# Attention and soft-MoE in one kernel: q and k loaded in four-row pieces plus a rest, in place of nine rows per partition

## The chip, the cores and the metric

One core of a Trainium2 chip runs the whole program. The metric is the device time of one execution in microseconds (us), the median of the runs shown. Beside it stands one execution under the hardware profiler, from which all durations below come.

## What is computed

There are 8 batches and 8 heads, 576 tokens and 16 beacon tokens per head, 64 channels per head. Attention is causal over the tokens, and the 16 beacon keys are open to all of them. Its output, 4608 rows of 512, goes through a soft mixture of experts with 8 experts of 4 slots and an inner width of 1024. Cut to what matters:

```
k_all = concat(beacon_k, k);  v_all = concat(beacon_v, v)        # 16 + 576 tokens
a = softmax(where(causal, -1e9, q @ k_all.T / 8))
x = (a @ v_all), heads side by side                              # (4608, 512)
logits = x @ phi                                                 # (4608, 32)
slot_input = softmax(logits, over tokens).T @ x                  # (32, 512)
slot_out[e] = relu(slot_input[e] @ w1[e]) @ w2[e]                # 8 experts
out = softmax(logits, over slots) @ slot_out                     # (4608, 512)
```

## The kernel before

The work has three stages. In the **attention stage** the loop of line 316 goes over 32 pairs of heads (n). In the **expert stage** (lines 385 to 399) the 32 slots go through the experts' two matrices. In the **output stage** (lines 405 to 420) the slot outputs are spread back over the 4608 rows.

The schedule is written out by hand: each engine runs its instructions in the order of the code. One iteration n of the attention loop issues, in this order: `score(n, 0)` and `score(n, 1)` (scores of pair n, exp on ScalarE at line 209, causal masks on GpSimd at lines 211 and 217), `transp(n + 1)`, `attend(n - 1, 0)`, `score(n, 2)`, `attend(n - 1, 1)`, `score(n, 3)`, up to three pieces of routing of the batch before (transposes of x, logits, slot inputs), then the loads: `load_pair(n + 5)`, a part of the next batch's v (`load_v`), casts of v (`cast_v`, odd chunks on VectorE, even chunks on GpSimd, line 244), and in two of three iterations from n = 3 on one piece of an expert's weights (`load_w`, from GpSimd's queue, line 119).

`load_pair` (line 83) brings q and k of two heads, each into a tile of 128 partitions of 9 rows of 64 fp32 values (`qf`, `kf`; the pool `qkp` has five buffers for each). Partition p holds rows 9p to 9p + 8 of the two heads' 1152 rows, so one DMA of 288 KB with one run of 2304 bytes per partition does it. These loads and those of v and the outputs go through SyncE's queue (SP), one after the other; a load into a buffer waits until TensorE has transposed what was there, five pairs earlier.

`transp` (line 181) takes the upper half of each fp32 value as bf16 and transposes it on TensorE, 18 matmuls of 64x64 for q and 18 for k, into a PSUM tile `tr` of the shape [128, 9, 64] (row within the partition, then partition). Then VectorE copies the tile to `qT` or `kT`, three buffers each, in which the columns are tokens in their natural order (line 190). The token 9s + j stands in PSUM at j * 64 + s, so this copy reads PSUM with a step of 64 elements and writes SBUF without gaps. GpSimd adds the 16 beacon columns to `kT` (line 193). The pool `ps_tr` has two buffers, which the routing pieces use as well.

`attend` (line 222) multiplies the masked exponentials by v and a column of ones, 15 matmuls into `av` (line 230). VectorE takes the reciprocal of the sums (line 237) and scales (line 238, into `xb`). The output tiles `osb` of line 406 use the slots of the weight tiles `w1h`, before and after the change.

Of the kernel before, what the change touches and what calls it, by code (L numbers as in the profile page):

```python
# [17 lines left out]
def kernel(  # L18
# [12 lines left out]
    nc = tc.nc  # L31
    P = 128
    B, H, S, D = q.shape
    Nb = beacon_k.shape[2]
# [7 lines left out]
    J = S // 64  # L42
# [40 lines left out]
    def load_pair(n):  # L83
        b, g = divmod(n, H // 2)
        for (d, src, nm) in ((qf, q, "qf"), (kf, k, "kf")):
            t = qkp.tile([P, J, D], FP, name=nm, tag=nm)
            nc.sync.dma_start(
                out=t[:, :, :],
                in_=src[b, 2 * g:2 * g + 2].rearrange("h s d -> (h s) d").rearrange(
                    "(p j) d -> p j d", j=J))  # L90
            d[n] = t

    vf = {}
# [14 lines left out]
    def load_w(m):  # L108
# [7 lines left out]
        else:  # L116
# [3 lines left out]
            out=d[e][:, o:o + 2048].rearrange("p (c f) -> p c f", c=c), in_=src)  # L120

    load_pair(0)
    bkf = const.tile([P, B, D], FP, name="bkf")
    nc.sync.dma_start(out=bkf[:, :, :], in_=beacon_k.rearrange("b h n d -> (h n) b d"))
    load_pair(1)
    load_v(0, 0)
    load_v(0, 1)
    load_v(0, 2)
    load_v(0, 3)
    phif = const.tile([P, NDC, NSL], FP, name="phif")  # L130
    nc.sync.dma_start(out=phif[:, :, :], in_=moe_phi.rearrange("(c p) e -> p c e", p=P))
    load_pair(2)
    load_pair(3)
    load_pair(4)
# [46 lines left out]
    def transp(n):  # L181
        for (f, dst) in ((qf, qT[n % 3]), (kf, kT[n % 3])):
            t = f.pop(n)
            tp = ps_tr.tile([P, J, 64], BF, name="tr", tag="tr")
            for j in range(J):
                for po in (0, 64):
                    hi = t[po:po + 64, j, :].bitcast(BF)[:, 1::2]
                    nc.tensor.transpose(tp[po:po + 64, j, :], hi,  # L188
                                        idb[po:po + 64, po:po + 64])
            nc.vector.tensor_copy(  # L190
                out=dst[:, Nb:Nb + S].rearrange("p (s j) -> p s j", j=J),
                in_=tp[:, :, :].rearrange("p j s -> p s j"))
        nc.gpsimd.tensor_copy(out=kT[n % 3][:, 0:Nb], in_=bkT[:, n, :])

    ex = {}
# [113 lines left out]
    nc.vector.tensor_copy(out=phih[:, :, :], in_=phif[:, :, :])  # L309
    beacons()  # L310
    transp(0)
    for c in range(NCH):
        cast_v(0, c)
    work = []
    wl = 0
    for n in range(NP + 1):
        b, g = divmod(n, H // 2)
# [4 lines left out]
        if n + 1 < NP:  # L322
            transp(n + 1)
# [81 lines left out]
    for cg in range(NG):  # L405
        osb = wh.tile([P, G, Dm], FP, name="osb", tag="w1h")
        dst = out[cg * P * G:(cg + 1) * P * G, :].rearrange("(p j) d -> p j d", j=G)
# [43 lines left out]
```

The softmax here doesn't subtract the row's maximum and nothing guards it: scores larger than these inputs give would overflow.

## Time and profile before

| what | value |
|---|---|
| runs | 251.77, 255.45, 257.04 us; median 255.45 |
| the profiled execution | 257.04 us, of which the span from first to last instruction is 255.1 us |
| granted TensorE clock, mean | 0.853 of full speed |
| busy share of the span | TensorE 73%, its weight loads 52%, VectorE 52%, ScalarE 50%, GpSimd 34% |
| DMA packets | 63714, 55.63 MB |
| first transposes of pair 0; of pair 31 | at 16.2 us; at 177.7 us |
| expert stage; output stage | from about 196 us; from about 226 us |

The shares of busy time are means over the three stages. Times in the views count from the start of the span. Where a view gives a share of the DMA engines, it is the sum of the times that packets took, divided by 16 engines; packets of one engine overlap in part, so the share can be a little over 1.

### The profile page before, as it was taken

To read this page: it belongs to the slowest core of one execution; us is meant where nothing else is said; L and a number is where in the kernel's file an instruction comes from. 1 tells how busy PE (TensorE), PEld (TensorE's weight loads), DVE (VectorE), ACT (ScalarE), POOL (GpSimd) and SP (SyncE) were. 2 spreads that over 40 slices of the span, in tenths; PEclk is the share of its full clock that TensorE was granted. 3 is DMA by queue.
4 is the path that set the end of the run, shared out by engine and by line. 5 is a ranking of instruction groups with operands and counts; after the bars stand their busy time and mean duration, and the time that the engine had idled before them with its cause. 6 is when DMAs were issued, how large, how long until landed. Compare 5 with 4: busy or idle time off the path is not lost.

```text
span 255.1 us, 8017 instructions
## 1 busy us (share of the span) xinstructions
PE 187.0 (73%) x3512; PEld 132.5 (52%) x3512; DVE 131.4 (52%) x304; ACT 128.3 (50%) x187; POOL 87.2 (34%) x161
## 2 busy tenths in 40 slices
PE   0038877778876777788878798798867999967770
PEld 0036655657755656566666666577566445521110
DVE  6055656755766756664576557556543000035651
ACT  0108677675675666656567556756821000025550
POOL 4024445442454434625244353432460440000000
PEclk9999999997999999779799659958967579985555
DMA  7999779999999999979989999173579999908997
GB/s 218 215 315 256 188 210 247 287 249 236 237 230 215 194 285 233 263 222 231 217 236 206 240 185 268 25 106 61 85 114 202 192 180 202 190 6 364 408 403 301
DMA packets 63714, 55.63 MB, mean 218 GB/s; under 512 B 41920, under 2 KB 50112, under 8 KB 62656
## 3 DMA queue, kind: packets, MB, share of 16 engines
q1 hardware_dynamic: 50880, 38.35, 52.0%
q0 software_dynamic: 12800, 16.78, 40.6%
q8 instruction: 27, 0.44, 0.7%
q14 instruction: 7, 0.06, 0.1%
HBM read 62.46 MB, written 9.44 MB: 282 GB/s over the span
## 4 chain that ended last, share of the span: by engine, by line
PE 54%; DVE 30%; ACT 6%; SPq 3%; issue 3%; DMA 2%
PE av L230 12%; PE tr L188 7%; PE av L397 7%; PE sc_155 L203 6%; PE tr L272 4%; DVE xb_142 L238 4%; PE tr L257 4%; DVE xb_141 L238 4%; PE sc_154 L411 3%; PE sc_154 L203 3%; PE tr L392 3%; DVE osb L415 3%; DVE qT_129 L190 3%; ACT osb L414 2%; ACT ex L209 2%
## 5 line engine op out<-in xcount | busy, mean ns | idle before, releaser
L209 ACT ACTIVATE ex<-sc_154 128x1024 f16<-128x1024 f32 x64 | 63.0, 984 | 41.9 <-PE sc_154 L203 41.8
L211 POOL TENSOR_SCALAR_AFFINE_SELECT ex<-ex 128x1024 f16<-128x1024 f16 x32 | 34.8, 1087 | 86.7 <-ACT ex L209 86.7
L230 PEld LDWEIGHTS <-ex 128*128 128x128 f16 (+2 forms) x960 | 42.8, 113 | 33.1 <-issue 31.6
L209 ACT ACTIVATE ex<-sc_155 128x992 f16<-128x992 f32 x64 | 48.4, 756 | 21.5 <-PE sc_155 L203 21.5
L230 PE MATMUL av<-vh_137,ex 128*128 128x65 f16 (+2 forms) x480 | 24.4, 209 | 11.5 <-DVE xb_141 L238 11.5
L230 PE MATMUL av<-vh_138,ex 128*128 128x65 f16 (+2 forms) x480 | 23.0, 203 | 13.1 <-DVE xb_142 L238 12.2
L397 PE MATMUL av<-w2h,hTz 128*32 128x512 f16 x64 | 18.6, 443 | 2.3 <-ACT hTz L395 2.3
L188 PE MATMUL tr<-idb,kf 64*64 64x64 bf16 x576 | 17.3, 209 | 0.8 <-DVE bkT L175 0.4
L188 PE MATMUL tr<-idb,qf 64*64 64x64 bf16 x576 | 17.5, 211 | 0.0
L188 PEld LDWEIGHTS <-qf 64*64 64x64 bf16 x576 | 13.7, 123 | 7.0 <-issue 5.7
L188 PEld LDWEIGHTS <-kf 64*64 64x64 bf16 x576 | 14.9, 124 | 1.5 <-issue 1.0
L395 ACT ACTIVATE hTz<-tr 128x32 f16<-128x32 f32 x8 | 1.6, 197 | 27.3 <-PE tr L392 27.3
L401 DVE TENSOR_SCALAR soh<-av,rd 32x512 f16<-32x512 f32 x1 | 0.7, 740 | 27.5 <-PE av L397 27.5
L119 POOL DMA_DIRECT2D w1h<-in_moe_w_dram x16 | 11.5, 722 | 9.7 <-PE tr L392 9.7
L411 PEld LDWEIGHTS <-eLh 32*128 32x128 f16 x36 | 4.5, 124 | 18.0 <-issue 17.6
L411 PE MATMUL sc_154<-soh,eLh 32*128 32x512 f16 x18 | 8.6, 576 | 6.9 <-DVE osb L415 6.1
L119 POOL DMA_DIRECT2D w2h<-in_moe_w_dram x16 | 12.0, 756 | 4.4 <-PE av L397 4.4
L190 DVE COPY qT_128<-tr 128x576 bf16<-128x576 bf16 x11 | 8.3, 756 | 9.9 <-PE tr L188 9.8
L190 DVE COPY qT_129<-tr 128x576 bf16<-128x576 bf16 x11 | 8.3, 756 | 8.7 <-PE tr L188 8.6
L190 DVE COPY qT_130<-tr 128x576 bf16<-128x576 bf16 x10 | 7.6, 756 | 9.6 <-PE tr L188 9.6
L172 PE MATMUL tr<-idb,bkd 128*128 128x128 bf16 x8 | 1.0, 311 | 15.3 <-DVE bkd L169 15.3
L414 ACT ACTIVATE osb<-sc_154,rc 128x512 f32<-128x512 f32 x9 | 6.2, 687 | 11.9 <-PE sc_154 L411 11.9
(207 smaller groups left out, 327.7 us busy)
## 6 DMA issues: line engine op xcount, KB each, us to landing
qf<-in_q_dram SPq DMA_DIRECT2D x32, 288.0 KB, 4.7
kf<-in_k_dram SPq DMA_DIRECT2D x32, 288.0 KB, 5.2
w1h<-in_moe_w_dram POOLq DMA_DIRECT2D x16, 512.0 KB, 8.2
w2h<-in_moe_w_dram POOLq DMA_DIRECT2D x16, 512.0 KB, 8.1
out_dram<-osb SPq DMA_DIRECT2D x8, 1024.0 KB, 3.9
vf<-in_v_dram SPq DMA_DIRECT2D x24, 256.0 KB, 6.3
vf<-in_v_dram SPq DMA_DIRECT2D x8, 224.0 KB, 5.4
vf<-in_v_dram SPq DMA_DIRECT2D x8, 160.0 KB, 6.7
```

Of the source, the lines that this page charges most:

```text
L119: nc.gpsimd.dma_start(out=d[e][:, o:o + 2048].rearrange("p (c f) -> p c f", c=c), in_=src)
L188: nc.tensor.transpose(tp[po:po + 64, j, :], hi, idb[po:po + 64, po:po + 64])
L190: nc.vector.tensor_copy(out=dst[:, Nb:Nb + S].rearrange("p (s j) -> p s j", j=J), in_=tp[:, :, :].rearrange("p j s -> p s j"))
L203: nc.tensor.matmul(sc[0:kn, a, col:col + un], kT[n % 3][64 * a:64 * a + 64, P * c:P * c + kn], qT[n % 3][64 * a:64 * a + 64, u0:u0 + un], ...
L209: nc.scalar.activation(ex[n][:, :, o:o + w], sc[:, :, 0:w], AF.Exp, scale=scale)
L211: nc.gpsimd.affine_select(out=ex[n][:, :, 0:512].rearrange("p a (c t) -> p a c t", c=4), in_=ex[n][:, :, 0:512].rearrange("p a (c t) -> p ...
L230: nc.tensor.matmul(av[0:m, a, i * DD:(i + 1) * DD], ex[n][0:kn, a, o:o + m], vh[b % 2][0:kn, c, h, :], start=(c == 0), stop=(c == i))
L238: nc.vector.tensor_tensor(out=xb[b % 2][:, :, h, :], in0=avv[:, :, 0:D], in1=r5[:, :].unsqueeze(2).broadcast_to([P, NCH, D]), op=AL.mult)
L257: nc.tensor.transpose(tp[:, ii, t, 0:m], xb[b % 2][0:m, i, 2 * t:2 * t + 2, :].rearrange("p h d -> p (h d)"), idh[0:m, 0:m])
L397: nc.tensor.matmul(sop[0:NSL, 0, :], hTz[:, e, t, :], w2h[e][:, t * Dm:(t + 1) * Dm], start=(e == 0 and t == 0), stop=(e == E - 1 and t == ...
L411: nc.tensor.matmul(fp_[:, a, :], etok(cg, jj + a), soh[:, :], start=True, stop=True)
L414: nc.scalar.activation(osb[:, jj, :], fp_[:, 0, :], AF.Copy, scale=rc[:, i:i + 1])
```

## The change

Each of q and k of a pair now comes in three DMAs in place of one. The first two bring 512 rows of one head each to 64 partitions: partition p gets rows 4p to 4p + 3 and 256 + 4p to 256 + 4p + 3, two runs of 1 KB. The third brings the last 64 rows of both heads, one row of 256 bytes per partition: on the DRAM side its pattern is 2 heads x 64 rows x 64 values, on the SBUF side 128 partitions x 64 values. The matmuls of the transposes stay the same. The copy out of PSUM becomes two: one of 512 columns, which reads PSUM without gaps in runs of 64 and writes every fourth bf16 element (a step of 8 bytes), and one of the last 64 columns, without gaps on both sides.

```diff
         for (d, src, nm) in ((qf, q, "qf"), (kf, k, "kf")):
             t = qkp.tile([P, J, D], FP, name=nm, tag=nm)
-            nc.sync.dma_start(
-                out=t[:, :, :],
-                in_=src[b, 2 * g:2 * g + 2].rearrange("h s d -> (h s) d").rearrange(
-                    "(p j) d -> p j d", j=J))
+            for a in range(2):
+                hs = src[b, 2 * g + a]
+                nc.sync.dma_start(
+                    out=t[64 * a:64 * a + 64, 0:8, :].rearrange("p (c j) d -> p c j d", j=4),
+                    in_=hs[0:512].rearrange("(c p j) d -> p c j d", p=64, j=4))
+            nc.sync.dma_start(out=t[:, 8, :],
+                              in_=src[b, 2 * g:2 * g + 2, 512:S, :])
             d[n] = t
...
             nc.vector.tensor_copy(
-                out=dst[:, Nb:Nb + S].rearrange("p (s j) -> p s j", j=J),
-                in_=tp[:, :, :].rearrange("p j s -> p s j"))
+                out=dst[:, Nb:Nb + 512].rearrange("p (c s j) -> p c j s", c=2, j=4),
+                in_=tp[:, 0:8, :].rearrange("p (c j) s -> p c j s", j=4))
+            nc.vector.tensor_copy(out=dst[:, Nb + 512:Nb + S], in_=tp[:, 8, :])
```

## The prediction

> **What bounds the kernel now.** I read the page first. Its chain of work that ended last belongs to TensorE and VectorE; DMA has 2% of it.
>
> ```profile
> PE 54%; DVE 30%; ACT 6%; SPq 3%; issue 3%; DMA 2%
> L190 DVE COPY qT_128<-tr 128x576 bf16<-128x576 bf16 x11 | 8.3, 756 | 9.9 <-PE tr L188 9.8
> ```
>
> The chain in order of time shows one pair (columns: start, us, what):
>
> ```profile
> 101.30 0.76 DVE qT_130 L190
> 102.06 0.66 DVE kT_133 L190
> 102.72 0.11 DVE r_2245 L237
> 102.83 0.02 issue
> 102.86 0.50 DVE xb_142 L238
> 103.36 0.04 issue
> 103.40 0.67 PE av L230 x15
> ```
>
> The copies of q and k stand ahead of the reciprocal and the scaling, and the second `attend` waits for the scaling. The waits say that this happens in all 31 such iterations (15 + 16), 23.7 us in total:
>
> ```profile
> PE av L230 <- DVE xb_142 L238: 12.2, 15, 1.0
> PE av L230 <- DVE xb_141 L238: 11.5, 16, 1.0
> ```
>
> So VectorE's copies lie on the path, and loads don't. SP's own waits, and the table of stretches (columns: stretch, us, busy PE, PEld, DVE, ACT, POOL with counts, granted clock, DMA share, GB/s) tell how near the loads are:
>
> ```profile
> SPq L87 <- PE tr L188: 78.7, 25, 5.7
> ```
>
> ```profile
> 20.00:60.00 40.00, 31.51 (x731) 24.87 (x731) 23.99 (x56) 28.15 (x38) 18.42 (x35) 0.97 0.99 240
> 60.00:100.00 40.00, 30.47 (x730) 24.02 (x725) 26.16 (x64) 27.03 (x39) 18.45 (x35) 0.99 1.07 239
> 100.00:140.00 40.00, 33.03 (x747) 26.32 (x743) 24.97 (x58) 26.12 (x38) 17.28 (x33) 0.87 1.00 226
> ```
>
> SP waits for buffers (so loads are ahead), but the last column but one, the DMA engines' share, stands at 0.99 to 1.07: little is free. Part of that is queueing. From the trace's DMA packet records I take service times of one engine: 256-byte packets (v) 19 ns, from the fullest 2.5 us (2,080 packets on 16 engines; median record 18); 2304-byte packets (q, k) 93 ns (median); weight packets 80 ns (w1 and w2 alternate: 503 packets of one kind in 2.5 us) and 155 ns (258 of the other). Mixed full stretches come out at 93 to 100% with these prices.
>
> Work of one engine until the last q/k has landed: q/k 64 tiles x 8 packets x 93 = 47.6 us; v and beacons 38,912 packets / 16 x 19 = 46.2 us; 16 weight pieces issued by then (8 x 32 x 80 + 8 x 16 x 155 ns) = 40.3 us. Sum 134 us of the 158 us between 2 and 160 us. The pairs' transposes start every 5.2 us (16.2 to 177.7 us, 31 steps); the last loads are in some 20 us before use.
>
> [...] Every pattern of the kernel before starts with 128, 112, 80 or 16, all multiples of 16; the trace has no other[...]. [...] copies without gaps out of PSUM take 160, 214, 314 and 687 ns for 32, 128, 320 and 1024 elements (0.53 ns each after some 145 ns), while line 190 with its read step takes 752 ns, 145 + 576 x 1.05. [...]
>
> **The change, part by part.**
>
> VectorE: the 512-element copy writes with a step of 4, so 145 + 512 x 1.05 = 683 ns; the rest 145 + 64 x 0.53 = 179 ns[...]. That is 862 in place of 752 ns busy. But successive instructions overlap by some 75 ns (the copy of q above starts at 101.30 and takes 0.758, that of k starts at 101.97), so on the path a tile costs 608 + 104 in place of 677: +35 ns. Times 62 tiles: +2.2 us, at most 62 x 110 ns = +6.8 us without overlap. [...] TensorE's matmuls are unchanged; the waits for a tile's three DMAs fall on different transposes, and I put them at nothing: covered by loads that are in 20 us early; if late, the whole PE queue behind, `attend` included, stands.
>
> SP: 6 issues per pair for 2, at 0.33 to 0.43 us: +1.6 us per pair of SP, hidden in the 78.7 us of waiting. SP's records show eight completion semaphores used in turn, so at most eight loads are in flight; the pair's 7.25 loads fit its 5.2 us as long as one lands in under 8 / 7.25 x 5.2 = 5.7 us (before: 4.7 to 6.7, for whole tiles). v, next in SP's queue, goes out 1.6 us later; GpSimd already waits three times for its fifth chunk (6.6 us), so 0 to 3 us may come from there. At the start eight more issues precede phi, whose landing at 14.3 us lets VectorE begin: +1 us, up to +2.4 us.
>
> DMA engines: a 1 KB packet lies on the line through 18, 93 and 159 ns (256, 2304, 4096 bytes): 46 ns[...]. The two head loads: 256 packets, 16 per engine, 0.736 us, about what one load costs now (0.744). The rest is the point: 128 packets of 256 bytes with a DRAM pattern that starts with 2. [...] it runs on 2 engines, 64 packets each: 64 x 19 = 1.216 us on those two, nothing on the others. (Spread over 16 it would be 0.152 us.)
>
> So the two engines have to do, until the last q/k: 64 x (0.736 + 1.216) = 124.9, v 46.2, weights 40.3: 211.4 us in place of 134. Start at 2, landing about 1 us after the last packet: 214.4 us. It is consumed at 177.7 in the kernel before: +36.7 us. Per pair: 2 x 1.952 + 1.44 + 1.68 = 7.0 us against the 5.2 us at which TensorE consumes. The lead of five pairs lasts until about pair 9 (loaded at 2 + 5 x 3.9 + 6.7 for the first v, + 2 x 5.35 + 3 x 7.0 = 60 us; its transposes start at 59 us). From there on VectorE's +35 ns are hidden under waiting for loads (left: ten pairs, under 1 us). What follows the last pair (18 us of attention tail, experts, outputs) stays. [...] two groups of line 397 take 3.6 us where the granted clock is low and 1.9 where it is high, so I take off 3 us.
>
> Sum against the profiled execution: span 255.1 + 36.7 - 3 = 289, 257.04 gives 291. The median of the runs is 1.6 us lower: 255.45 + 34 = 289; I say 288. [...]
>
> **Rivals.**
>
> A, the rest spreads over 16 engines[...] Then the start (+2.4), VectorE (+2.2) and late v (+2) give 262. [...]
>
> B, not slower: the rest spreads over 16 engines[...]: 64 x 0.888 + 46.2 + 40.3 = 143 us, hidden. Left are VectorE's 2.2 and the start's 1: 258.5. It decides at the number of engines that the rest uses: the room is 178 - 3 - 134 = 41 us, the rest takes 155.6 / k us, so from k = 4 on it is hidden. For it: every DMA in this trace uses 16. Against: the pattern of DRAM can't be merged, as the heads are 576 rows apart.
>
> C, faster: [...] (145 + 271 = 416 ns): on the path 341 + 104 for 677, 62 x 232 ns = 14 us less, with loads hidden: 241. Against: step 4 on the write side.
>
> **How the numbers follow.** The likeliest 0.66 at 288, own range 264 to 303; A 0.09 at 262; B 0.20 at 258.5, 256 to 262; C 0.05 at 241. What a measurement of this kernel can tell from no change is about 2%, 5.1 us: 250.3 to 260.6. Slower by over 2%: 0.66 + 0.09 + 0.05 of B = 0.80; within: 0.15 of B; faster: 0.05. The range leaves out C, the lower part of B and the top of the likeliest: 258 to 303.
>
> **What would show it.** In the profile after: waits of `tr` (line 188) for DMA `qf`/`kf`, from about pair 9 on, of over 1 us per pair; transposes some 6.5 to 7 us apart in the second half; the last near 214 us; the DMA share in these stretches well under 1, as 14 engines idle; two copies of some 680 and 180 ns in line 190. Wrong if `tr` doesn't wait for DMA at all (B), if the large copy takes near 420 ns (C), or if the wait is there with the DMA share at 1 (A).

## The result and the profile after

The changed kernel takes 314.97 us, the median of 4 runs (313.11 to 317.47), beside 255.76 us for the kernel before (4 runs, 251.77 to 257.04). The ratio is 1.243, with a 95% interval of 1.221 to 1.264. Ratios with an interval, here and below, are taken from the undisturbed executions alone, so they differ a little from the quotients of the medians. The profiled execution took 314.24 us, its span 312.3 us against 255.1. In this section "after" is that execution.

Where the 57.2 us lie, read from the starts of the transposes as in the prediction: the first comes at 20.95 us instead of 16.22 (+4.7), the pairs are 6.88 us apart instead of 5.21 (31 steps, +51.7), and what follows the last start takes 78.2 us instead of 77.4 (+0.8). So nearly all is in the attention loop.

The page's chain of work that ended last has moved from TensorE towards VectorE and DMA, and the copies are two kinds (the columns after the bar: busy us, mean ns, idle before):

```profile
PE 40%; DVE 36%; DMA 10%; SPq 4%; ACT 4%; issue 3%; POOL 1%
...
L193 DVE COPY qT_148<-tr 128x512 bf16<-128x512 bf16 x11 | 14.4, 1309 | 10.9 <-PE tr L191 10.8
```

The copy of 512 columns takes 1309 ns; the copy of all 576 took 756. The chain in order of time shows a pair after the change (start, us, what):

```profile
142.17 0.64 PE tr L191 x18
142.81 0.02 issue
142.83 1.30 DVE qT_148 L193
144.14 0.03 DVE qT_148 L196
144.16 1.14 DVE kT_151 L193
145.30 0.02 DVE kT_151 L196
145.33 0.05 DVE r_2483 L241
145.38 0.02 issue
145.40 0.50 DVE xb_161 L242
145.90 0.04 issue
145.94 1.04 PE av L234 x15
```

The sequence is that of the pair that the prediction shows, but the two copies hold the path for 1.30 + 0.03 + 1.14 + 0.02 = 2.49 us where they held it for 0.76 + 0.66 = 1.42. The rest copies (L196, 221 ns each) overlap the next instruction almost wholly. The second thing to see is the last line: the 15 matmuls take 1.04 us where before's chain has 0.67, with the same instructions.

Summed over the loop, from the first transposes of pair 0 to those of pair 31, the chain has 74.1 us of copies of q and k where it had 31.1 (+43.0), 95.8 us of TensorE where it had 88.6 (+7.2), and 9.9 us of waiting for v where it had none; its other parts shrank. So in the changed kernel itself most of what the path gained lies in the copies.

The waits (times in us: total, count, longest) show the lengthened wait for the scaling, and a grown one, of GpSimd for v. First GpSimd's of the kernel before, then those after the change:

```profile
POOL vh_137 L244 <- DMA vf<-in_v_dram: 5.2, 2, 3.9
...
POOL vh_138 L244 <- DMA vf<-in_v_dram: 1.4, 1, 1.4
```

```profile
POOL vh_158 L248 <- DMA vf<-in_v_dram: 33.8, 10, 6.4
POOL vh_157 L248 <- DMA vf<-in_v_dram: 31.5, 8, 6.7
...
PE av L234 <- DVE xb_162 L242: 24.8, 15, 3.4
PE av L234 <- DVE xb_161 L242: 23.7, 16, 2.0
...
PEld L191 <- DMA qf<-in_q_dram: 1.2, 4, 0.3
```

The wait for the scaling doubled (23.7 to 48.5 us). GpSimd waits 65.3 us for v, where it waited 6.6. The transposes hardly wait for q and k at all, 1.2 us in the whole run: the wait that the prediction rests on isn't there.

The table of stretches (columns as in the prediction) says that TensorE ran at a lower granted clock and that the DMA engines were less busy, not more:

```profile
20.00:60.00 40.00, 28.87 (x526) 22.73 (x527) 25.72 (x54) 19.99 (x24) 14.27 (x27) 0.73 0.72 170
60.00:100.00 40.00, 29.18 (x496) 22.38 (x494) 23.89 (x53) 18.32 (x26) 13.55 (x24) 0.67 0.86 173
100.00:140.00 40.00, 28.88 (x567) 22.46 (x566) 25.79 (x60) 20.81 (x30) 14.15 (x26) 0.74 0.82 179
```

Finally SP's issues, by line (min/median/max in ns, then first and last start in us). First of the kernel before, then of the changed one:

```profile
L87 SPq DMA_DIRECT2D qf<-in_q_dram x32: 327/328/1553, 0.8 to 151.0; - x32
```

```profile
L89 SPq DMA_DIRECT2D qf<-in_q_dram x64: 595/624/3552, 0.8 to 208.5; - x64
L92 SPq DMA_DIRECT2D qf<-in_q_dram x32: 534/541/810, 2.3 to 209.3; - x32
```

A head load holds SP for 0.6 us and sometimes for over 3. From SP's records of start and duration: before, 114 loads keep SP busy for 63.8 us of the 155 until the last issue, and in the gaps it waits for buffers. After, 242 loads keep it busy for 196.7 us of 214.4, and its gaps of more than 0.15 us sum to 1.2 us. SP has become a full queue; v, which stands in it behind six loads of q and k, is what comes late.

### The profile page after: what moved, and what is told of

It reads as the page before. It is cut to its first block, busy times and chain, and to the rows that moved or that the text cites. A ratio compares the mean times of both kernels' runs of the same rounds, so it can differ in the third digit from the quotient of the medians.

```text
span 312.3 us, 8209 instructions
## 1 busy us (share of the span) xinstructions
PE 214.2 (69%) x3512; PEld 153.0 (49%) x3512; DVE 164.7 (53%) x368; ACT 129.4 (41%) x187; POOL 88.3 (28%) x161
## 4 chain that ended last, share of the span: by engine, by line
PE 40%; DVE 36%; DMA 10%; SPq 4%; ACT 4%; issue 3%; POOL 1%
PE av L234 9%; PE sc_175 L207 6%; DMA w2h<-in_moe_w_dram 6%; PE tr L191 5%; PE tr L276 5%; DVE qT_149 L193 5%; PE tr L261 4%; DVE qT_148 L193 4%; DVE kT_152 L193 4%; DVE qT_150 L193 4%; DVE kT_151 L193 4%; DVE kT_153 L193 4%; PE sc_174 L207 3%; DVE xb_162 L242 3%; DMA vf<-in_v_dram 3%; DVE xb_161 L242 3%
## 5 line engine op out<-in xcount | busy, mean ns | idle before, releaser
L234 PEld LDWEIGHTS <-ex 128*128 128x128 f16 (+2 forms) x960 | 50.1, 126 | 58.3 <-issue 56.6
L234 PE MATMUL av<-vh_157,ex 128*128 128x65 f16 (+2 forms) x480 | 29.0, 228 | 23.7 <-DVE xb_161 L242 23.7
L234 PE MATMUL av<-vh_158,ex 128*128 128x65 f16 (+2 forms) x480 | 25.9, 216 | 24.9 <-DVE xb_162 L242 24.8
L193 DVE COPY qT_149<-tr 128x512 bf16<-128x512 bf16 x11 | 14.4, 1306 | 14.5 <-PE tr L191 14.4
L191 PEld LDWEIGHTS <-qf 64*64 64x64 bf16 x576 | 16.0, 138 | 9.2 <-issue 7.6
L193 DVE COPY qT_148<-tr 128x512 bf16<-128x512 bf16 x11 | 14.4, 1309 | 10.9 <-PE tr L191 10.8
L191 PE MATMUL tr<-idb,qf 64*64 64x64 bf16 x576 | 20.1, 227 | 0.0
L193 DVE COPY qT_150<-tr 128x512 bf16<-128x512 bf16 x10 | 13.1, 1309 | 12.9 <-PE tr L191 12.9
L401 PE MATMUL av<-w2h,hTz 128*32 128x512 f16 x64 | 17.1, 412 | 3.7 <-ACT hTz L399 2.3
L191 PE MATMUL tr<-idb,kf 64*64 64x64 bf16 x576 | 19.2, 223 | 0.4 <-DVE bkT L178 0.4
L248 POOL CAST vh_158<-vf 128x512 f16<-128x512 f32 (+1 forms) x12 | 7.4, 614 | 33.9 <-DMA vf<-in_v_dram 33.8
L191 PEld LDWEIGHTS <-kf 64*64 64x64 bf16 x576 | 16.6, 139 | 0.6 <-issue 0.5
L248 POOL CAST vh_157<-vf 128x512 f16<-128x512 f32 (+1 forms) x12 | 7.3, 614 | 31.5 <-DMA vf<-in_v_dram 31.5
L276 PE MATMUL tr<-xT,phih 128*32 128x288 f16 x64 | 15.1, 403 | 0.4 <-DVE xT L266 0.4
L193 DVE COPY kT_151<-tr 128x512 bf16<-128x512 bf16 x11 | 14.1, 1285 | 0.0
L193 DVE COPY kT_152<-tr 128x512 bf16<-128x512 bf16 x11 | 14.1, 1284 | 0.0
```

What stands on the lines that cost most here:

```text
L191: nc.tensor.transpose(tp[po:po + 64, j, :], hi, idb[po:po + 64, po:po + 64])
L193: nc.vector.tensor_copy(out=dst[:, Nb:Nb + 512].rearrange("p (c s j) -> p c j s", c=2, j=4), in_=tp[:, 0:8, :].rearrange("p (c j) s -> p c ...
L234: nc.tensor.matmul(av[0:m, a, i * DD:(i + 1) * DD], ex[n][0:kn, a, o:o + m], vh[b % 2][0:kn, c, h, :], start=(c == 0), stop=(c == i))
L248: (nc.vector if c % 2 else nc.gpsimd).tensor_copy(out=vh[b % 2][0:kn, c, :, 0:D], in_=vf[(b, c)][0:kn])
L276: nc.tensor.matmul(lp[0:NSL, 0:w], phih[:, t, :], xT[b][:, t, Nb + hf * w:Nb + (hf + 1) * w], start=(t == 0), stop=(t == NDC - 1))
L401: nc.tensor.matmul(sop[0:NSL, 0, :], hTz[:, e, t, :], w2h[e][:, t * Dm:(t + 1) * Dm], start=(e == 0 and t == 0), stop=(e == E - 1 and t == ...
```

## The experiments

My theory after the result: two causes, the copies and SP's full queue, each of which alone costs most of the 57 us, so that either hides behind the other. The rivals: the copies alone; the two DMA engines of the rest loads, as predicted; loads over 64 partitions. The experiments ran in several groups, each with its own runs of the kernel before; the ratios are to those.

### The copies

**m1_copy_forms**: the kernel before, with 22 extra copies of 128 x 512 bf16 ahead of the loop, two of each of eleven forms. It is there for the forms' times; its own, 273.76 us in one run, says nothing.

```diff
+            nc.vector.tensor_copy(out=mbi[:, :], in_=src)
+            nc.vector.tensor_copy(out=flat[:, 0:1024].rearrange("p (n t) -> p n t", t=2)[:, :, 0], in_=src)
+            nc.vector.tensor_copy(out=flat[:, 0:2048].rearrange("p (n t) -> p n t", t=4)[:, :, 0], in_=src)
+            nc.vector.tensor_copy(out=flat[:, 0:4096].rearrange("p (n t) -> p n t", t=8)[:, :, 0], in_=src)
...
```

> The kernel before with 22 more copies of 512 bf16 elements per partition at its start, each form twice: out of PSUM without gaps to SBUF with a write step of 1, 2, 4, 8 elements; the changed kernel's form; its turned form; SBUF to SBUF with a write step of 4; SBUF to SBUF with a read step of 4; PSUM to fp32; and two on ScalarE (write step 4, and 1). Theory 'write step': 0.41 us without gaps, 1.3 us for write step 4 whatever the source, ScalarE too or not is open; turned form 0.68 us. Rival 'source': the changed form is slow because of its PSUM read order or its four-part pattern; then the plain write step of 4 takes 0.68 us and only the changed form 1.3 us.

Measured, from the groups of instructions. `tr` is the PSUM tile, `mbi` and `w1h` lie in SBUF; L186 writes without gaps, L187, L188 and L189 every second, fourth and eighth element; L191 reads PSUM with a step and writes without gaps; L192 is L188 with its source in SBUF; L195 is L188 on ScalarE, L196 the gapless copy there:

```profile
L189 DVE COPY w1h<-tr 128x512 bf16<-128x512 bf16 x2 | 4.8, 2419 | 0.1
...
L195 ACT COPY w1h<-tr 128x512 bf16<-128x512 bf16 x2 | 2.6, 1294 | 8.6 <-DVE mbf L194 8.6
L188 DVE COPY w1h<-tr 128x512 bf16<-128x512 bf16 x2 | 2.6, 1290 | 0.1
...
L192 DVE COPY w1h<-mbi 128x512 bf16<-128x512 bf16 x2 | 1.5, 734 | 0.1
L187 DVE COPY w1h<-tr 128x512 bf16<-128x512 bf16 x2 | 1.4, 718 | 0.0
L191 DVE COPY mbi<-tr 128x512 bf16<-128x512 bf16 x2 | 1.4, 690 | 0.1
L196 ACT COPY mbi<-tr 128x512 bf16<-128x512 bf16 x2 | 1.4, 684 | 0.0
...
L186 DVE COPY mbi<-tr 128x512 bf16<-128x512 bf16 x2 | 0.8, 424 | 3.2 <-ACT mbi L196 3.1
```

Out of PSUM the time grows with the step of the write: 424, 718, 1290, 2419 ns for steps 1, 2, 4, 8. The changed kernel's own order of columns, which has step 4 too, took 1502 ns here (L190) and 1296 on average in the kernel. From SBUF the same write with step 4 takes 734, and out of PSUM a step on the read side with a gapless write takes 690. So my 683 ns was the price of a step on the read side; both expectations, of 1.3 us from any source and of 0.68 us, missed one case each.

**e1_gapless_write**: the changed kernel with its large copy turned round, PSUM read with the step and SBUF written without gaps. The loads stay.

```diff
-                out=dst[:, Nb:Nb + 512].rearrange("p (c s j) -> p c j s", c=2, j=4),
-                in_=tp[:, 0:8, :].rearrange("p (c j) s -> p c j s", j=4))
+                out=dst[:, Nb:Nb + 512].rearrange("p (c s j) -> p c s j", c=2, j=4),
+                in_=tp[:, 0:8, :].rearrange("p (c j) s -> p c s j", j=4))
```

> The changed kernel, with the copy of 512 columns turned round: it reads PSUM with a step of 64 elements and writes without gaps. Loads stay as changed. Theory 'copies' (the write step of 8 bytes makes the copy 1.3 us and the copy sets the pair's time): the copy takes 680 ns, the pairs come at 5.3 us again, and 255 + 5 (start) + 2 (copies) = 262 us. Theory 'loads' (the rest on two DMA engines sets the pair's time, as predicted): the last q/k still lands near 214 us, TensorE waits for it, and 214 + 78 us of what follows = 292 us.

Measured: 304.67 us, ratio 1.213 (1.202 to 1.223). The copy takes 686 ns and the pairs are still 6.56 us apart. With shorter copies GpSimd only waits longer for v, and the chain through the loop (20.68 to 224.03 us) now runs over v's loads for a third of the time, 69.3 us:

```profile
POOL vh L248 <- DMA vf<-in_v_dram: 91.7, 19, 8.5
```

```profile
by line: DMA vf<-in_v_dram 34.1%; PE sc L207 9.0%; PE av L234 7.0%; DVE qT L193 5.3%; PE tr L191 5.1%; DVE kT L193 5.0%; DVE xb L242 4.4%; SPq L89 4.2%; PE tr L261 3.9%; PE tr L276 3.8%; POOL ex L215 3.0%; issue 2.3%; SPq L92 1.9%; POOL vh 
```

So the loads alone cost some 53 us, more than either side expected.

**e2_copies_alone**: the kernel before with the two new copies and its own loads. Here the nine rows of a partition aren't in the order that the copies assume, so the tokens in `qT` and `kT` are permuted; the work is the same.

```diff
-                out=dst[:, Nb:Nb + S].rearrange("p (s j) -> p s j", j=J),
-                in_=tp[:, :, :].rearrange("p j s -> p s j"))
+                out=dst[:, Nb:Nb + 512].rearrange("p (c s j) -> p c j s", c=2, j=4),
+                in_=tp[:, 0:8, :].rearrange("p (c j) s -> p c j s", j=4))
+            nc.vector.tensor_copy(out=dst[:, Nb + 512:Nb + S], in_=tp[:, 8, :])
```

> The kernel before with its loads, and the changed kernel's two copies out of PSUM. Tokens of q and k then stand in another order than the causal mask assumes. Theory 'copies': each copy 1.3 us, + 1.1 us per pair on the path, 31 x 1.1 = 34: 289 us, up to 307 if the lower TensorE clock of the changed kernel comes from these waits. Theory 'loads': 258 to 262 us.

Measured: 304.22 us, ratio 1.211 (1.197 to 1.225), 6.58 us a pair. SP is busy for 57.4 us only and v never comes late; the wait for the scaling is what is left:

```profile
PE av L231 <- DVE xb L239: 47.5, 31, 2.0
```

So the copies alone also cost some 52 us. Together the two parts cost 59: they overlap. I read this so: a pair that waits for its copies gives SP time (GpSimd waits 65.3 us for v with both parts and 91.7 with the loads alone), and a pair that waits for v gives VectorE time.

The copies' 1.07 us a pair more on the path would make 33 us in 31 pairs. The traces show more: from the first transposes to those of pair 31 it is 203.9 us with the copies alone and 161.4 before, 42.5 more. (That isn't 52 because the trace of before is of the slowest of its four runs, and this one of the fastest of its four.) The chain through this stretch, 15.53 to 219.46 us:

```profile
by line: DVE qT L190 19.4%; DVE kT L190 17.3%; PE sc L204 12.9%; PE av L231 12.3%; DVE xb L239 8.6%; PE tr L188 7.5%; PE tr L258 6.1%; PE tr L273 4.4%; ACT ex L210 2.6%; issue 2.3%; PE tr L296 2.1%; DVE r L238 1.2%; DVE xT L263 1.0%; DVE qT
```

With the short rest copies the copies are 76.7 us of it: those of all pairs. In the same stretch of before they are 31.1 us: the chain went through the copies of some 22 pairs, and in the others something else set the time. So the longer copies also hold pairs that they hadn't held. TensorE's part of the chain grew from 88.6 to 92.2 us only.

TensorE's clock was lower too. In the trace of before, one `attend` of 15 matmuls takes 0.46 us from first to last start, or 0.80 where the granted clock is one half. The share of the slow ones is 0.20 before, 0.47 with the copies alone, 0.34 with the loads alone, 0.48 after. In the records of before and after the granted clock is 0.5 or 1.0 only, in 16 and 38 stretches, and all but the last stretch of each last 3.4 us or a multiple of it; what makes the clock change I haven't worked out from them. TensorE's busy time rose from 187.0 us to 206.2 with the copies alone and to 214.2 after, with the same instructions. How much of the lost time is the clock's wasn't tried by itself.

### The loads: how many, and on how many engines

**e3_rest_by_head**: the changed kernel with each rest load split by head, so that it starts with 64 rows; 8 loads of q and k a pair. **e4_both_mended** is that with the copy of e1_gapless_write.

```diff
-            nc.sync.dma_start(out=t[:, 8, :],
-                              in_=src[b, 2 * g:2 * g + 2, 512:S, :])
+            for a in range(2):
+                nc.sync.dma_start(out=t[64 * a:64 * a + 64, 8, :],
+                                  in_=src[b, 2 * g + a, 512:S, :])
```

> The changed kernel, with the load of the last 64 rows cut into two DMAs, one per head, each of 64 partitions, so that 16 engines share each. Theory 'copies': the copies still hold the pairs at some 6.4 to 6.9 us, start 6 us later than before: 295 to 315 us. Theory 'loads': the DMA work per pair falls from 7.0 to 4.9 us, TensorE no longer waits for it: 262 us.

> Both edits: the copy that writes without gaps, and the rest loaded per head. Both theories: near the kernel before, 255 + 6 (start, eight loads per pair at 0.6 us of SP) + 2 (copies) = 263 us. If it stays above 275, something else in the loads costs: SP's issue time (8 x 0.6 = 4.8 us of a pair's 5.2), late v[...].

Measured: 343.06 us (ratio 1.366, 1.354 to 1.377) and 334.57 us (1.334, 1.323 to 1.345). Both are far slower than with the loads that they replace, where I had expected the rest on 16 engines to help (it does run on 16: of the 70336 packets on SP's queue 65280 are data, and the other 5056 are 316 DMAs x 16); only for e4_both_mended had I left open that something else in the loads might cost. What grew is the number of loads, 306 for 242. SP was in issues for 214 us of 242 and 240; its gaps of more than 0.15 us sum to 9.2 and 7.6 us.

**e8_extra_on_two** and **e7_extra_by_head_16**: the kernel before, plus rest loads into tiles that nothing reads, in the form with two heads (64 more loads), or split by head (128 more).

```diff
             d[n] = t
+            pt = qkp.tile([P, D], FP, name="pt", tag="pt", bufs=8)
+            nc.sync.dma_start(out=pt[:, :], in_=src[b, 2 * g:2 * g + 2, 512:S, :])
```

> The kernel before, with its own loads and copies, and two more loads per pair that nobody reads: the last 64 rows of both heads of q and of k into scratch, in the form that the changed kernel uses (2 heads x 64 rows, on two DMA engines). Theory 'two engines': those two get 7.0 us of work per pair, the last q/k lands near 214 us, 214 + 77 = 291 us or more. Theory 'SP's queue': SP has 1.6 + 2 x 0.55 = 2.7 us per pair, under the pair's 5.2, so 252 to 258 us.

> The same bytes as in the run beside it, per head: four more loads per pair, each on 16 engines. Theory 'two engines': one engine has 4.6 us of work per pair, nothing waits: 252 to 258 us. Theory 'SP's queue': SP has 1.6 + 4 x 0.65 = 4.2 us per pair and holds eight loads in flight where a pair has 7.25; v goes out later: 258 to 275 us.

Measured: 283.85 us (ratio 1.125, 1.112 to 1.139) and 288.62 us (1.141, 1.128 to 1.155). Each alone, with the copies and q/k loads of before, costs 30 to 35 us. Neither is in a case that I had named: e8_extra_on_two lies between its two, e7_extra_by_head_16 above both. Beside before's 50880 packets on SP's queue and the 8192 of the extra rows, the first has 128 more, 64 x 2 engines, and the second 2048, 128 x 16. In the first, 54 of SP's issues take over 1 us, 101.7 us in sum; in the second 27, 45.4 us. So the two-engine form does hold SP longer per load, but spreading it in twice as many loads is no better.

**e5_rest_by_batch_16**: gapless copies, and the rest of a whole batch's heads in two loads of q and two of k, once per four pairs: 210 loads, all of a form that starts with 64 rows.

```diff
+            if g == 0:
+                rt = qkp.tile([P, H // 2, D], FP, name=nm + "r", tag=nm + "r", bufs=2)
+                rows = src[b].rearrange("(g a) s d -> a s g d", a=2)
+                for a in range(2):
+                    nc.sync.dma_start(out=rt[64 * a:64 * a + 64, :, :], in_=rows[a, 512:S])
...
```

> The changed kernel with the copy that writes without gaps, and the last 64 rows loaded once per batch: two DMAs each for q and k (one per head parity, 64 partitions x 4 pairs, 16 engines). Per pair SP has 4 + 1 + 1.25 issues, 3.9 us, and no engine more than 5 us of work. Theories 'two engines' and 'SP's queue' both: 255 + 3 (start) + 2 (copies) = 260, up to 268. If it stays above 275, the loads to 64 partitions cost by themselves[...].

Measured: 282.47 us (277.59 to 283.15), beside 253.78 for the kernel before; there is no interval for this ratio. It is 22 us under e1_gapless_write, and still outside the 260 to 268 us that I expected. For a time above 275 us I had blamed loads over 64 partitions; nothing here separates that from the rest: SP has 153.4 us of issues and 14.1 us of gaps up to 181.4 us, and the DMA engines' share from 20 us on to there is 1.02, as high as before.

**e12_rest_side_by_side**: gapless copies; each rest load is walked row first into a tile of 64 partitions by two heads. The number of loads and the bytes are those of the changed kernel, but the outermost count is 64 and not 2; a tensor has 17 transposes in place of 18. All of SP's 252 DMAs now run on 16 engines: the small packets that announce landings number 4032, 252 x 16, where e1_gapless_write has 3136.

```diff
-            nc.sync.dma_start(out=t[:, 8, :],
-                              in_=src[b, 2 * g:2 * g + 2, 512:S, :])
+            rt = qkp.tile([64, 2, D], FP, name=nm + "r", tag=nm + "r")
+            nc.sync.dma_start(out=rt[:, :, :],
+                              in_=src[b, 2 * g:2 * g + 2, 512:S, :].rearrange("a s d -> s a d"))
...
```

> The kernel with gapless copies and the changed loads (304.7 us), with one thing other: each rest load is walked row first into a tile of 64 partitions by two heads side by side, so that its outermost count is 64 instead of 2. It is the same 242 loads and the same bytes; its transposes are 17 instead of 18 a tensor. If the two engines of the rest set the pace: its packets spread over 16 engines, SP's 73 us of issues over 1 us shrink to about 45, and it goes to 273 to 285 us, 5.5 to 5.8 us a pair, as with the rest once per batch. If the number of issues on SP sets the pace: 298 to 305 us and 6.4 to 6.6 us a pair.

Measured: 301.19 us, ratio 1.199 (1.187 to 1.211), against 1.213 (1.202 to 1.223) with the two engines: the intervals overlap, and the time is in the second case that I had named. The issues over 1 us did shrink as expected, from 73.2 to 41.8 us, but 16.7 us of gaps came in their place, nearly all (15.4 us) ending just after the load eight places earlier had landed. The two engines aren't what set the pace.

Put side by side, from SP's records (loads; us in issues; end of the last issue; us from one pair to the next; the last column is the time from the first issue to the end of the last, divided by the loads):

| kernel | copies | loads | in issues | last ends | per pair | per load |
|---|---|---|---|---|---|---|
| before | of before | 114 | 63.8 | 155.0 | 5.21 | SP waits for buffers |
| e8 (two engines) | of before | 178 | 177.6 | 192.1 | 6.07 | 1.07 |
| e7 | of before | 242 | 162.1 | 196 | 6.11 | 0.81 |
| e5 | gapless | 210 | 153.4 | 181.4 | 5.72 | 0.86 |
| e12 | gapless | 242 | 170.0 | 204.2 | 6.48 | 0.84 |
| e1 (two engines) | gapless | 242 | 192.8 | 210.3 | 6.56 | 0.87 |
| after (two engines) | new | 242 | 196.7 | 214.4 | 6.88 | 0.88 |
| e4 | gapless | 306 | 214.2 | 240.2 | 7.44 | 0.78 |
| e3 | new | 306 | 213.9 | 241.9 | 7.65 | 0.79 |

In every kernel but the first SP is busy, or held by eight loads in flight, from its first load to its last; a load costs SP 0.8 to 0.9 us all in, 1.07 in one; and the pairs are as far apart as SP's queue lets them be (for after, 214.4 / 32 = 6.7 us against 6.88). This is an agreement of records, not a test: it doesn't separate SP's own time from that of the DMA engines, whose share in e5 is 1.02.

### v's place in the queue

**e9_v_first** puts v's load ahead of those of q and k in each iteration. **e10_v_two_early** issues v's loads two iterations earlier, and **e11_batch_rest_v_early** does that to e5. All have gapless copies; the edit shown is that of e10_v_two_early. In e9_v_first the edit also moved the casts of v under the condition of `load_pair`, which no longer holds in iteration 27: the last two chunks of the last batch's v are never cast (38 casts of v in the trace instead of 40). It leaves out work, so I give its time no weight.

```diff
-            if b + 1 < B:
-                load_v(b + 1, g)
+            b2, g2 = divmod(n + 2, H // 2)
+            if b2 + 1 < B:
+                load_v(b2 + 1, g2)
```

> The changed kernel with the copy that writes without gaps, and in each iteration v's load ahead of those of q and k in SP's queue. If only v's lateness (it has the least lead) set the 304 us of the same kernel with v last, then q and k use up their lead of five pairs instead: the last q/k still lands near 212 us, 212 + 78 = 290 us. If SP or the DMA engines had room, 262 us. If the order does nothing, 304 us.

> The kernel with the gapless copies and the changed loads (304.7 us, GpSimd waits 91.7 us for v), with each of v's loads issued two iterations earlier; bytes, forms and number of issues are unchanged. If the kernel with the new loads is slow because v, with the least lead, comes late behind a long queue: v's waits go under 15 us and the time goes to 262 to 270 us. If SP's queue (193 us of issues in 210) or the two engines of the rest are themselves the limit: v's waits move to qf and kf, the last load packet stays near 212 us, and the time stays at 290 to 305 us.

> The kernel with the gapless copies and the rest once per batch over 16 engines (282.5 us, GpSimd waits 53.1 us for v, SP busy 153 of 181 us), with each of v's loads two iterations earlier. If v's lateness is all that is left: 258 to 266 us with v's waits under 15 us. If the loads' pace itself (SP's queue, or loads over 64 partitions) holds it: above 273 us, with waits for qf or kf in place of v's.

Measured: 298.62 us; 298.07 us (ratio 1.187, 1.176 to 1.198); 274.01 us (1.093, 1.084 to 1.102). In e10_v_two_early an early v gains 6.6 us on e1_gapless_write; e11_batch_rest_v_early is 8.5 us under the median of e5 and 3.6 under its fastest run. Both times are in the case that I had named for the pace of the loads, but the waits are not: GpSimd still waits 89.8 and 53.0 us for v, and the transposes of e10_v_two_early some 10 us for q and k. Why, SP's records show: in e10_v_two_early, SP issues the load of pair n + 5 some 20 us after that pair's buffers came free, where it was about 7 us in e1_gapless_write, 5 to 6 us after the change, and under 1 us before. The lead that v got, SP's growing lag ate. So lead alone isn't the cause; the pace at which SP gets its loads out is. e11_batch_rest_v_early is the nearest to before of all with 64-partition loads, and there the engines are filled, as its stretch from 20 to 180 us shows (share 1.06, 208 GB/s, against 1.02 and 233 before):

```profile
20.00:180.00 160.00, 121.41 (x2681) 94.88 (x2678) 96.02 (x282) 98.52 (x136) 66.94 (x124) 0.89 1.06 208
```

More engine time for fewer bytes could be the price of loads over 64 partitions; it isn't separated from queueing here, and here the engines may hold the pace as well as SP.

**e13_side_by_side_v_early**: e12_rest_side_by_side with v two iterations earlier.

> The same with v's loads two iterations earlier. If the queue only lags by a few us and v has the least lead, it goes to 262 to 270 us. If the pace of the loads is still the limit, it gains less than 8 us over the run without the early v, and the lag of SP behind its slots grows above 10 us as it did in the two earlier runs with the early v.

Measured: 293.77 us, ratio 1.173 (1.162 to 1.184): 7 us less than without, as the second case said, and SP's lag grew from about 7 us to about 20 in the second half.

**e14_v_on_scalar_queue** takes v off SP: its 48 loads are issued by ScalarE, with gapless copies. **e15_after_v_on_scalar** does it to the changed kernel. **e16_v_scalar_early** and **e17_after_v_scalar_early** add the two iterations.

```diff
-            nc.sync.dma_start(out=vf[(b, c)][p0:p0 + hi - lo],
+            nc.scalar.dma_start(out=vf[(b, c)][p0:p0 + hi - lo],
...
```

> The kernel with gapless copies and the changed loads (304.7 us), with the 48 loads of v issued by ScalarE instead of SP. Bytes and engines are the same. If SP's queue is what holds the load phase (0.79 to 0.87 us a load, all in, in five kernels): SP keeps 194 loads, 154 to 169 us, and v no longer stands behind them; 5.2 to 5.5 us a pair, 258 to 270 us. If the DMA engines hold it: v still comes late, above 290 us.

> The changed kernel itself (315.0 us) with v's loads issued by ScalarE. If its two causes hide each other, little is gained: with SP's cause taken away it stands where the copies alone stood, 300 to 308 us. If the copies are of little weight beside the loads: 265 to 280 us.

> The run with v issued by ScalarE (309.3 us), v two iterations earlier. There SP no longer ran behind (0.7 us behind its slots), but ScalarE came to v's loads so late that each was cast 5 to 9 us after its issue. With two iterations more, some 12 us, v is there: if SP's queue and v's lead together were the whole of the loads' cost, 5.2 to 5.5 us a pair and 256 to 268 us. If the DMA engines themselves are too slow for this form of loads: above 285 us, with waits for qf, kf or v of over 40 us.

> The changed kernel (315.0 us) with v issued by ScalarE and two iterations earlier. If its loads then cost nothing more, what is left is the cost of the copies: 298 to 308 us, 6.5 to 6.6 us a pair, as with the copies alone. If the two causes add up instead of hiding each other: 265 to 280 us.

Measured: 309.34 us (ratio 1.211, 1.192 to 1.230), 327.08 (1.274, 1.253 to 1.294), 307.06 (1.218, 1.211 to 1.226), 318.19 (1.258, 1.247 to 1.269). Nothing was gained. e15_after_v_on_scalar and e17_after_v_scalar_early miss both of their cases. e14_v_on_scalar_queue and e16_v_scalar_early have times of the case in which the DMA engines hold the loads, but the engines' share from 20 us to SP's last load is 0.86 in both, against 0.83 in e1_gapless_write: they aren't full. SP did come free: from the load of pair 13 on it is less than 1 us behind its buffers in e14_v_on_scalar_queue. But each move put another wait in. In e14_v_on_scalar_queue ScalarE comes to v's loads only behind its exps, so most are cast some 4 to 10 us after their issue and GpSimd waits:

```profile
POOL vh L248 <- DMA vf<-in_v_dram: 77.6, 18, 7.5
```

In e16_v_scalar_early v is in time, and GpSimd's masks wait for ScalarE instead:

```profile
POOL ex L217 <- ACT ex L215: 139.1, 32, 9.7
...
ACT ex L215 <- DMA kf<-in_k_dram: 11.6, 2, 7.8
```

Its records name the reason. Both queues take the same eight completion semaphores in turn, so most issues of v on ScalarE first wait until a load of q or k that SP issued some 4 to 9 us before has landed, and the exps stand behind them (four of their waits, 22.1 us in sum, are put down to loads of q and k: the 11.6 us above and 10.5 for `qf`). So these runs show where v may not go; they don't show what the kernel would take with SP relieved and nothing else touched.

### A version that beats both

**b1_k_behind_attend** keeps the loads and the copy of before and moves k's transposes and copy behind the first `attend`, so that the reciprocal and the scaling no longer stand behind both copies.

```diff
-            transp(n + 1)
+            transp_q(n + 1)
         if n >= 1:
             attend(n - 1, 0)
+        if n + 1 < NP:
+            transp_k(n + 1)
```

> The kernel before with one order changed: q is transposed and copied ahead of the first attend as before, k's transposes and copy come behind that attend, so that on VectorE the reciprocal and the scaling stand ahead of k's copy. If VectorE's copies are on the path through that wait,[...] 31 x 0.7 = 21 us go: 228 to 240 us. If the copy is only moved to another wait (k is needed at the next scores): 250 to 256 us.

Measured: 243.58 us, ratio 0.970 (0.963 to 0.976), 4.80 us a pair: faster, and between my two cases. The wait for the scaling falls from 23.7 us to 6.9, and GpSimd's for v is next:

```profile
POOL vh L253 <- DMA vf<-in_v_dram: 20.5, 9, 5.5
PE av L239 <- DVE xb L247: 6.9, 22, 2.5
```

## Why the prediction was wrong

The direction was right; 288 us and the range up to 303 were too low, and the mechanism was another. By its steps:

**What bounds the kernel before**: right in the main. The copies lie on the path, and e2_copies_alone and b1_k_behind_attend both show it. But the waits for the scaling in all 31 iterations don't mean that the copies set the time of every pair: the chain goes through those of some 22.

**VectorE, "+35 ns" a tile: the first step that failed.** It took the price of a step on the read side, 145 + 512 x 1.05 = 683 ns, for a write with a step of 4. It takes 1296 ns. (The rest copy takes 221 ns for my 179.) The overlap with the next instruction was as I said, so where the copies were on the path it got 1.07 us longer a pair, 33 us in 31 pairs instead of 2.2, and they came to be on it in every pair. The copies alone cost 52 us. The step had a bound on each side, but both came from rows that write without gaps; no row of before showed the form at all. The doubt was on the other side, rival C.

**SP, "+1.6 us per pair, hidden in the 78.7 us of waiting": the second.** The issues were priced by the old form, 0.33 to 0.43 us. The head loads take 0.60 to 0.62 us, the rest 0.53, and 38 issues over 1 us sum to 75.9 us. All issues come to 196.7 / 32 = 6.1 us a pair; before they came to 63.8 / 32 = 2.0, of the 5.2 us that a pair has. The cover was real, 78.7 / 32 = 2.5 us a pair, but 4.1 us more don't fit under it. The condition on eight loads in flight held up in part: that limit shows where all loads run on 16 engines (e5, e11 and e12 wait 14 to 17 us for it); with the two engines SP is held in the issues first (196.7 us of them after, and 1.2 us of gaps). (The 4.7 to 6.7 us to landing were medians of groups; single loads of q and k before took 2.7 to 8.4 us.)

**DMA engines, "two engines have 7.0 us a pair": its number came true and its reason did not.** The rest does run on two engines: the small packets that announce landings number 3136, which is 188 x 16 + 64 x 2 (178 other loads and 10 issues of outputs, and 64 rest loads); a 1 KB packet took 46 ns as estimated; and the last packet went at 216.6 us where 214.4 us was predicted for the landing. No trace had shown this ahead of the result: the 124 DMAs on SP's queue in the kernel before have 1984 small packets, 16 each. But the transposes waited 1.2 us for `qf`, not over 1 us a pair; the last of them came at 234.1 us, 17.5 us after the last packet; and spreading the rest over 16 engines left the time within its interval. The last packet comes then because SP is done with its last load only at 214.4 us; that this is the predicted time is luck.

**v, "0 to 3 us"**: GpSimd waits 65.3 us for v after, and 91.7 us with gapless copies. I had asked what the six loads do to q and k, which have five pairs of lead, and not to v, which has the least.

**The start, "+1, up to +2.4"**: +4.7 us. It is 20.7 us with the changed loads alone and 15.5 with the copies alone, so it belongs to the loads.

**The clock, "-3"**: that it would be higher after the loop was my estimate, and the sign was wrong. The expert and output stages gained nothing (+0.8 us), and the attention stage's granted clock fell from 0.91 (20 to 155 us) to 0.70 (20 to 214 us).

**The rivals**: none came true. A needed a DMA share at 1 (it was 0.72 to 0.86), B hidden loads, C a large copy of 416 ns (it took 1296). That loads over 64 partitions are slower, which A assumed, and the packet prices behind both ends of my range, 264 and 303, were shown by no trace. A and B shared both steps that failed, and C the one on SP, which is why the range couldn't reach 315.

**What stays open**: how much the kernel would take with SP's queue relieved and nothing else moved; how much of the time the lower clock costs; what part of an issue over 1 us goes with the form of the load and what part, if any, with full engines (the loads of before have them too: 13 of 114 in the kernel before, and 28, 55.2 us in sum, in b1_k_behind_attend, whose engines' share is 1.08 from 20 us to SP's last load); and whether loads over 64 partitions cost engine time of their own. That more loads on SP go with more time is seen with gapless copies (210, 242, 306 loads: 282, 301 to 305, 335 us), though e8_extra_on_two, with rest loads on two engines, takes 284 us with 178 loads and e7_extra_by_head_16 289 us with 242; that SP's queue is the whole of the loads' cost is argued from its records.

## What to carry to other kernels

Price an operation by a row with the same step on the same side of the same memories; if there is none, you have no upper bound for its cost yet. When a load is cut into several, add up the issuing queue's time per iteration, all in, and ask which load behind it has the least lead: a queue that waits half the time is cover for so many issues and not for any number. Two changes that cost 52 and 53 us alone cost 59 together here, so undoing one of them shows next to nothing of its weight: measure each alone on the kernel before.

## What the hardware showed that I had not expected

- A copy of 512 bf16 values out of PSUM takes 424, 718, 1290 and 2419 ns when it writes SBUF with a step of 1, 2, 4 and 8 elements; from SBUF, step 4 takes 734 ns. ScalarE out of PSUM takes 684 ns without gaps and 1294 with step 4.
- A load of two runs of 1 KB into each of 64 partitions holds SP for 0.60 us at least, one of a single run of 2304 bytes into each of 128 partitions for 0.33; after the change 38 of 242 issues held it for 1 to 3.6 us.
- Loads issued by ScalarE and by SP took the same eight completion semaphores in turn, so that ScalarE's queue waited for SP's loads (in e16_v_scalar_early, for some that SP had issued 4 to 9 us before).
- The same instructions on TensorE took 187.0 us of busy time before and 214.2 after; the granted clock during the loads was 0.91 before (20 to 155 us) and 0.70 after (20 to 214 us).
